# A second staging tile for V, and a new order of work, in a fused attention and gated-unit kernel

## The chip, the cores and the metric

One core of one Trainium2 chip runs the whole program. The metric is the device time of one execution in microseconds (us), median over several runs. The names of the engines in the profile are PE (TensorE, matrix products; PEld is its weight load), DVE (VectorE), ACT (ScalarE), POOL (GpSimd) and SP (SyncE, which here issues the DMA transfers; SPq is its queue). "Clock" is the mean clock that TensorE was granted, as a share of full speed.

## The reference, cut to what matters

Eight batches, eight heads, 576 positions, head size 64; then a gated unit with a causal convolution of five taps over 512 channels.

```python
def _attn_ref(q, k, v, s):                     # (8, 8, 576, 64), s: (8, 8, 576)
    scores = np.matmul(q, k.transpose(0, 1, 3, 2)) / np.sqrt(D)
    cum = np.cumsum(np.maximum(s, 0.0), axis=-1)
    bias = -(cum[:, :, :, None] - cum[:, :, None, :])
    scores = np.where(causal, -1e9, scores + np.minimum(bias, 0.0))
    ...                                        # softmax
    return np.matmul(attn, v)

def _moe_ref(x, w_val, conv_w, w_out):         # x: (8, 576, 512)
    for k in range(5):
        gate_pre += conv_w[k] * xp[:, k:k + S, :]
    gate = 1.0 / (1.0 + np.exp(-gate_pre))
    return gate * (x @ w_val) @ w_out
```

## The kernel before

The kernel is a list of some thousand small tasks. Each names its engine, a planned duration, a key and the tasks it needs. When the kernel is built, a planner runs the list through a simple model of the engines, always taking the ready task with the lowest key; the order that comes out is the order in which the instructions are written. In the traces each engine works off its own list in that order (ScalarE's 204 instructions stand line by line as planned) and waits where an operand is missing. So a planned duration costs no time by itself. It only decides the order.

```python
    def run(self):                             # the planner
        ...
                if e == "SP":
                    idle_at[e] = now + 0.06                    # issuing a transfer is planned as 0.06 us
                    dma_free = max(dma_free, now + 1.2) + us   # one transfer after the other
                    t["done"] = dma_free + 0.8
                else:
                    idle_at[e] = t["done"] = now + us
        ...
    plan = Plan(dict(P=3, gp=2, th=6, ot=3, qkf=3))            # ot: three output tiles
    ...
    vst = one.tile([128, NKB, 8, 65], FP32, name="vst")        # the one staging tile for V
    ...
    def vprime(eng, b, p):                                     # V of two heads, scaled, to bf16
        h = slice(2 * p, 2 * p + 2)
        eng.tensor_tensor(Vps[b % 2][:, :, h], vst[:, :, h], w[...], ALU.mult)

    def load_v_pair(p):                        # first batch: three transfers for two heads
        for h in (2 * p, 2 * p + 1):
            nc.sync.dma_start(out=vst[:, 0:4, h, 0:64], in_=v[0, h, 0:512, :].rearrange("(i p) d -> p i d", i=4))
        nc.sync.dma_start(out=vst[64:128, 4, HP[p], 0:64], in_=v[0, HP[p], 512:576, :].rearrange("h s d -> s h d"))

    def load_v_block(b, i):                    # later batches: five transfers for eight heads
        n = kbs[i]
        nc.sync.dma_start(out=vst[128 - n:128, i, :, 0:64], in_=v[b, :, kbo[i]:kbo[i] + n, :].rearrange("h s d -> s h d"))
    ...
    plan.total = plan.run()
    with tc.manual_schedule():
        for t in plan.order:
            t["emit"]()
```

Positions 512 to 575 of Q and K (the "tail") are loaded apart from the rest, and the second and third block of scores of every pair of heads need them.

## Time and profile before

| | before |
|---|---|
| time, median of 3 runs | 210.72 us (209.64 to 211.25) |
| span of the profiled execution, clock | 209.3 us, 0.965 |
| busy PE / DVE / ACT / POOL | 175.4 / 178.0 / 163.1 / 161.9 us |
| start of the last evacuation of the output (ScalarE) | 203.44 us |

The prediction below shows the busy times, the chain and the three stretches. First, of the page's slices, TensorE's granted clock in forty equal slices (9 is 90% or more of full speed):

```profile
PEclk9999797599999999999999999999999999999995
```

```profile
12.00:18.00 6.00, 5.28 (x70) 3.94 (x67) 3.58 (x5) 5.62 (x9) 3.92 (x6) 1.00 1.09 265
...
33.00:39.00 6.00, 5.07 (x45) 2.99 (x45) 6.00 (x10) 3.55 (x6) 3.54 (x6) 0.60 1.08 260
```

From 40 to 190 us all four engines are 84% to 97% busy (busy time over the length of the stretch) and TensorE has 0.99 and 1.00 of its full clock.

### The profile page before, as it was taken

How to read it: one execution, taken by the hardware profiler on the slowest of the kernel's cores; microseconds unless marked ns; L12 is line 12 of the kernel's file. 1: busy time of each engine (PE TensorE's matmuls, PEld its weight loads, DVE VectorE, ACT ScalarE, POOL GpSimd, SP SyncE). 2: the span in 40 equal slices, each digit the busy share in tenths (PEclk: the TensorE clock that was granted, in tenths of full speed). 3: DMA queues.
4: the chain of work that ended last, by engine and by line, in shares of the span. 5: the costliest groups of instructions: out<-in, count | busy, mean ns of one | idle time of the engine just before them, and what ended most of it. 6: DMA issues, size and time to landing. Idle time of an engine off the chain costs nothing.

```text
span 209.3 us, 6007 instructions
## 1 busy us (share of the span) xinstructions
PE 175.4 (84%) x2392; PEld 119.4 (57%) x2411; DVE 178.0 (85%) x311; ACT 163.1 (78%) x205; POOL 161.9 (77%) x179
## 2 busy tenths in 40 slices
PE   1697885999969998689899799989899999979950
PEld 0455763475736766367665567565576556645620
DVE  3847969999888998669999999999999998999810
ACT  3279497778999899987996998799987998553330
POOL 4276486499959998999589999967975899999300
PEclk9999797599999999999999999999999999999995
DMA  4999999997999699999999821951149220222551
GB/s 147 238 279 288 361 147 216 354 271 207 244 281 323 138 319 221 323 297 226 222 383 307 190 107 25 184 147 49 54 110 219 81 77 1 99 104 75 180 180 61
DMA packets 69230, 40.48 MB, mean 193 GB/s; under 512 B 47109, under 2 KB 63493, under 8 KB 69194
## 3 DMA queue, kind: packets, MB, share of 16 engines
q1 hardware_dynamic: 69194, 40.01, 72.7%
q8 instruction: 21, 0.34, 0.7%
q14 instruction: 15, 0.12, 0.2%
HBM read 30.57 MB, written 9.44 MB: 191 GB/s over the span
## 4 chain that ended last, share of the span: by engine, by line
DVE 27%; ACT 24%; PE 23%; DMA 8%; issue 8%; SPq 7%; ACTq 0%; DVEq 0%
ACT P L592 13%; DVE gp L647 9%; PE banks L660 8%; DMA qkf<-in_moe_w_val_dram 6%; PE banks L672 6%; DVE xn L623 4%; PE banks L613 4%; ACT QKT L561 4%; ACT th L653 4%; DVE glu L666 3%; DVE gp L649 3%; PE banks L566 3%; SPq L515 3%; SPq L534 2%; ACT ot L677 2%
## 5 line engine op out<-in xcount | busy, mean ns | idle before, releaser
L592 ACT ACTIVATE P<-banks 128x1024 bf16<-128x1024 f32 x96 | 94.8, 1039 | 11.8 <-PE banks L566 9.9
L647 DVE SCALAR_TENSOR_TENSOR gp<-banks,ratio,gp 128x574 f32<-128x574 bf16 (+2 forms) x85 | 67.5, 804 | 2.4 <-POOL gp L645 1.7
L598 POOL TENSOR_SCALAR_AFFINE_SELECT P<-P 128x512 bf16<-128x512 bf16 x64 | 39.6, 640 | 11.3 <-ACT P L592 11.1
L566 PE MATMUL banks<-QKT 64*128 64x128 bf16 (+4 forms) x576 | 38.9, 249 | 8.8 <-ACT P L592 5.6
L660 PE MATMUL banks<-xT,wv 128*128 128x288 bf16 x256 | 41.7, 294 | 2.1 <-DVE glu L666 0.9
L672 PE MATMUL banks<-wo,glu 128*128 128x512 bf16 x141 | 38.3, 379 | 2.5 <-ACT QKT L561 0.8
L528 POOL TENSOR_TENSOR Vp<-vst,w 128x650 bf16<-128x650 f32 x29 | 37.6, 1316 | 1.3 <-DMA vst<-in_v_dram 1.3
L613 PE MATMUL banks<-Vp,P 128*128 128x65 bf16 x960 | 37.3, 198 | 1.3 <-ACT P L592 1.2
L613 PEld LDWEIGHTS <-P 128*128 128x128 bf16 x960 | 35.3, 101 | 5.4 <-issue 2.1
L566 PEld LDWEIGHTS <-QKT 64*128 64x128 bf16 x576 | 20.1, 97 | 27.0 <-issue 20.6
L653 ACT ACTIVATE th<-gp,halfw 128x576 f32<-128x576 f32 x32 | 25.2, 793 | 7.1 <-DVE gp L647 3.6
L660 PEld LDWEIGHTS <-wv 128*128 128x128 bf16 x256 | 22.8, 99 | 13.9 <-issue 6.1
L666 DVE SCALAR_TENSOR_TENSOR glu<-th,banks 128x288 bf16<-128x288 f32 x64 | 28.0, 445 | 1.1 <-PE banks L660 1.0
L623 DVE TENSOR_TENSOR xn<-banks,recs 128x640 bf16<-128x640 f32 x32 | 26.2, 818 | 0.3
L561 ACT COPY QKT<-banks 128x1024 bf16<-128x1024 bf16 x25 | 25.3, 1049 | 1.2 <-PE banks L557 1.1
L677 ACT COPY ot<-banks 128x512 f32<-128x512 f32 (+1 forms) x26 | 15.2, 587 | 11.4 <-PE banks L672 6.9
L672 PEld LDWEIGHTS <-glu 128*128 128x128 bf16 x160 | 14.6, 97 | 15.5 <-issue 2.7
L649 DVE SCALAR_TENSOR_TENSOR gp<-xT,ratio,banks 128x576 f32<-128x576 bf16 x25 | 20.1, 809 | 1.6 <-ACT xT L635 0.9
L644 POOL TENSOR_TENSOR tmp<-xT,ratio 128x576 f32<-128x576 bf16 (+3 forms) x18 | 20.6, 1142 | 1.0 <-ACT xT L635 0.5
L645 POOL TENSOR_TENSOR gp<-tmp,gp 128x573 f32<-128x573 f32 (+2 forms) x11 | 15.7, 1428 | 3.1 <-DVE gp L647 2.3
L631 PE MATMUL banks<-ident,xn 128*128 128x128 bf16 x160 | 14.2, 220 | 2.9 <-DVE xn L623 1.2
L518 POOL CAST qb<-qkf 128x2048 bf16<-128x2048 f32 x7 | 13.2, 1890 | 2.2 <-DMA qkf<-in_q_dram 2.2
(63 smaller groups left out, 169.2 us busy)
## 6 DMA issues: line engine op xcount, KB each, us to landing
out_dram<-ot SPq DMA_DIRECT2D x32, 256.0 KB, 2.9
qkf<-in_q_dram SPq DMA_DIRECT2D x7, 1024.0 KB, 8.5
qkf<-in_k_dram SPq DMA_DIRECT2D x7, 1024.0 KB, 9.9
vst<-in_v_dram SPq DMA_DIRECT2D x28, 256.0 KB, 5.4
vst<-in_v_dram SPq DMA_DIRECT2D x15, 128.0 KB, 4.0
first<-in_q_dram SPq DMA_DIRECT2D x4, 256.0 KB, 3.4
first<-in_k_dram SPq DMA_DIRECT2D x4, 256.0 KB, 3.4
tail<-in_q_dram SPq DMA_DIRECT2D x8, 128.0 KB, 8.7
```

Source lines behind the costliest of these rows:

```text
L528: eng.tensor_tensor(Vps[b % 2][:, :, h], vst[:, :, h], w[:, :, b * 8 + 2 * p:b * 8 + 2 * p + 2].unsqueeze(3).to_broadcast([128, NKB, 2, 65 ...
L561: copy[e](QKTs[b % 2][:, :, p, 0:512].rearrange("d w (x j) -> d w x j", j=4), slot["qt", b, p].rearrange("d w (j x) -> d w x j", j=4))
L566: nc.tensor.matmul(ps[:, hh, c0:c0 + nq], QKTs[b % 2][r, 1, p, k0:k0 + 128], QKTs[b % 2][r, 0, p, q0:q0 + nq], **kw)
L592: nc.scalar.activation(out=slot["Pt", n][:, :, step * 512:(step + 1) * 512], in_=slot["s", n, step], func=AF.Exp, scale=0.125)
L598: nc.gpsimd.affine_select(out=d, in_=d, pattern=[[0, 4], [1, 128]], compare_op=ALU.is_ge, fill=0.0, base=0, channel_multiplier=-1)
L613: nc.tensor.matmul(ps[:, hh, qb * 65:qb * 65 + 65], lhsT, Vps[b % 2][:, kb, 2 * p + hh, :], start=(kb == 0), stop=(kb == qb))
L623: nc.vector.tensor_tensor(xns[b % 2][:, :, p * 128:(p + 1) * 128].rearrange("t g (h d) -> t h g d", h=2), pv[:, :, :, 0:64], recs[:, n].un ...
L647: nc.vector.scalar_tensor_tensor(gp[:, o:S], slot["x", n][:, 0:S - o], r, gp[:, o:S], ALU.mult, ALU.add)
L653: nc.scalar.activation(out=th, in_=slot["g", n], func=AF.Tanh, scale=halfw[:, n % 4, :])
L660: nc.tensor.matmul(ps, wv[:, dc, c * 128:(c + 1) * 128], xTs[b % 2][:, dc, 2 + o:290 + o], start=(dc == 0), stop=(dc == 3))
L666: nc.vector.scalar_tensor_tensor(glus[b % 2][:, c, o], slot["t", n][:, o], 1.0, slot["v", n, hf], ALU.add, ALU.mult)
L672: nc.tensor.matmul(ps, glus[b % 2][:, c, WIN[i]:WIN[i] + 128], wo[:, c, :], start=(c == 0), stop=(c == 3))
```

## The change

Its intent: V of one batch can be loaded while that of the batch before is still being scaled, as there are two staging tiles. To make room, the second lies over five of the eight tiles of the first batch's Q and K. V of the second batch comes in pairs of heads, so that its scaling can begin early. The planner's durations for GpSimd come nearer to what the profile shows (that of VectorE for the first batch's V goes away from it, from 0.85 to 1.4 us, where the traces have 0.84), output tiles go from three to five, and all keys and choices of engine are searched anew under the new plan. The diff, cut to its core:

```diff
-DUE = dict(w=-69.33, lwv=-4.26, ...)
+DUE = dict(lv1=-0.54, lv1d=-8.43, vf=-76.23, lt=4.9, w=-131.75, ...)      # every key is new
-CHOICE = dict(vp0="0100", cast="12200210", te="10001100", ...)
+CHOICE = dict(tailc="2", vp0="0000", cast="01211201", te="00000000", ...)  # 0 and 1 choose the engine
...
-                    idle_at[e] = now + 0.06
                     dma_free = max(dma_free, now + 1.2) + us
+                    idle_at[e] = max(now + 0.06, dma_free - BEHIND)
...
-    plan = Plan(dict(P=3, gp=2, th=6, ot=3, qkf=3))
+    plan = Plan(dict(P=3, gp=2, th=6, ot=5, qkf=3))
...
-    vst = one.tile([128, NKB, 8, 65], FP32, name="vst")
+    vraw = [one.tile([128, NKB * 8 * 65], FP32, name=f"vst{j}") for j in range(2)]
+    vsts = [a.rearrange("p (i h d) -> p i h d", i=NKB, h=8) for a in vraw]
...
-                        f = slot["f", 0, wh, p] = one.tile([128, 2, 256], FP32, name=f"first{p}{wh}")
+                        f = slot["f", 0, wh, p] = (one.tile([128, 2, 256], FP32, name=f"first{i}") if i > 4 else
+                                                   vraw[1][:, i * 512:(i + 1) * 512].rearrange("p (h s) -> p h s", h=2))
...
+            if b == 1:
+                t = add("POOL", 0.7, DUE["vf"], lambda: v_frame(1), [T["cast", 0, i % 2, i // 2] for i in range(5)])
+                ts = [[add("SP", 1.45, DUE["lv1"] + DUE["lv1d"] * p, lambda p=p: load_v_pair(1, p), [t])] for p in range(4)]
...
-                T["vp", b, p] = add("POOL", 1.25, ...
+                T["vp", b, p] = add("POOL", 1.33, ...
-                t = add(("DVE", "POOL"), (0.73, 2.25), ... tap ...
+                t = add(("DVE", "POOL"), (0.73, 2.5), ... tap ...
```

## The prediction

> **What bounds the kernel now.** I read the page first, to see whether one engine is full; then the busy time by stretch, to see where the engines are not full; then the waits, for the ones that the change touches; and last the order of time at both ends. The first line below is the page's busy time, the second its chain by engine.
>
> ```profile
> PE 175.4 (84%) x2392; PEld 119.4 (57%) x2411; DVE 178.0 (85%) x311; ACT 163.1 (78%) x205; POOL 161.9 (77%) x179
> ...
> DVE 27%; ACT 24%; PE 23%; DMA 8%; issue 8%; SPq 7%; ACTq 0%; DVEq 0%
> ```
>
> No engine is full and no one engine owns the chain. VectorE (178.0 us of 209.3) and TensorE (175.4) are nearly level, and ScalarE and GpSimd are some 15 us behind. The busy time in three stretches (columns: stretch, length, then PE, PEld, DVE, ACT, POOL busy, clock, DMA share, GB/s) says where the missing 31.3 us of VectorE are:
>
> ```profile
> 0.00:40.00 40.00, 27.42 (x341) 19.59 (x341) 29.13 (x49) 26.29 (x35) 23.87 (x41) 0.89 0.97 249
> 40.00:190.00 150.00, 136.31 (x1989) 93.50 (x2006) 140.33 (x247) 131.14 (x163) 132.62 (x134) 1.00 0.72 186
> 190.00:210.00 20.00, 11.68 (x66) 6.31 (x65) 8.52 (x17) 5.64 (x9) 5.46 (x5) 0.87 0.38 130
> ```
>
> VectorE idles 10.9 us in the first 40, 9.7 in the 150 of the middle (94% busy) and some 11 in the end. So the middle is held by VectorE, with TensorE at 91%; the start by data (DMA share 0.97, and every engine a quarter to two fifths idle); the end by dependences. The waits that the change touches (who waited for what: total us, times, longest):
>
> ```profile
> ACT ot L677 <- DMA out_dram<-ot: 3.0, 2, 1.8
> ...
> DVE Vp L528 <- DMA vst<-in_v_dram: 2.0, 2, 1.3
> ...
> DVE wv L413 <- DMA qkf<-in_moe_w_val_dram: 1.9, 1, 1.9
> ...
> POOL Vp L528 <- DMA vst<-in_v_dram: 1.3, 2, 0.9
> ```
>
> The V staging tile costs its readers 3.3 us, 2.4 of them in the first 20 us. In the DMA queue's own list the single tile shows as well, since each load of V must wait until the batch before has been scaled, and what stands behind it waits too:
>
> ```profile
> SPq L540 <- POOL Vp L528: 6.9, 4, 2.1
> ...
> SPq L523 <- POOL Vp L528: 4.7, 3, 2.9
> ```
>
> In order of time, the fourth pair's Q (L515) is issued only at 11.97 us, because three V transfers stand between one pair's Q and K and the next pair's; and at the end ScalarE's last two evacuations wait for an output tile to be stored, after TensorE has ended at 201.79:
>
> ```profile
> 11.97 0.59 SPq L515 DMA_DIRECT2D first<-in_q_dram  x1
> ...
> 197.31 4.48 PE L672 MATMUL banks<-wo,glu 128*128 128x512 bf16 x19
> ...
> 201.08 0.59 ACT L677 COPY ot<-banks 128x512 f32<-128x512 f32 x1 [1.26 <-DMA out_dram<-ot]
> 203.44 0.59 ACT L677 COPY ot<-banks 128x512 f32<-128x512 f32 x1 [1.77 <-DMA out_dram<-ot]
> ```
>
> [...] a pair of V takes 1.28 us on GpSimd and 0.84 on VectorE, and a tap takes 1.14 + 1.43 = 2.57 us there and 0.80 here, as it is two instructions there. [...] the trace has one scaling of 2.26 us against a median of 1.28, beside the 2.12 us conversion of the weights on VectorE[...]
>
> **The change part by part.** The kernel's arithmetic, bytes and matrix products stay. What changes is which engine does an operation, in which order, and how long a buffer is held. The planner runs when the kernel is built and only fixes the order, so its constants cost no time themselves.
>
> *Engines.* Counted from the strings of choices, times this trace's means. VectorE: one scaling of V more, +0.84; one first conversion less, -0.42; the first tail's conversion, -0.41; three tail evacuations, -1.27; one Q/K evacuation, -1.22; seven x evacuations (26 to 19), -3.16; two output evacuations (14 to 12), -1.37; three taps more, as GpSimd's fall from 18 to 15, +2.41. Sum -4.6: 178.0 becomes 173.4. ScalarE gets the counterparts: two conversions 1.24, three tails 1.78, one Q/K 1.05, seven x 4.65, two outputs 1.17. Sum +9.9: 163.1 becomes 173.0. GpSimd: one V less -1.28, three taps less -7.7, one conversion less -0.61 and the first tail's more +0.61, the memsets of the second V tile +0.7 (0.16 + 0.52 in the start of this trace). Sum -8.3: 161.9 becomes 153.6. TensorE stays at 175.4. So the fullest engine falls from 178.0 to 175.4, and three engines now stand within 2.5 us of each other. In the middle, where VectorE is 94% busy, I take its 4.6 us less at about half, -2.5 us, because TensorE at 91% and ScalarE with 9.9 us more soon bind in its stead.
>
> *The end.* Output tiles go from three to five. With the two waits gone (1.26 + 1.77), the last evacuation can start when TensorE has ended, 201.8 instead of 203.44. That is on the path that ends last: -1.6 us.
>
> *The start.* In the old order twelve V transfers of 0.47 to 0.63 us on the queue stand among the eight of Q and K. The new keys put all Q and K first (-10.8 to -0.2) and V behind (1.8 to 2.9), so eight issues of about 0.5 us bring the fourth pair's K about 6 us earlier than 12.61. ScalarE's exponentials, spread out until about 29 us now, can be packed closer. Against that the tail's two transfers go ahead of the first Q (about 0.6 us later). The second batch's V comes in twelve transfers in place of five, seven more at about 0.55 = 3.9 us of queue time, in a stretch where DMA is full anyway, and it is asked for early: 1.18 MB more ahead of the value weights is 4.7 us at 249 GB/s, and the first gated product needs those weights. Net I take -2.5 of the 10.9 idle us.
>
> *The second V tile in the middle.* It frees loads from the batch before, but the readers wait only 0.9 us there. The 11.6 us of queue waits are prefetch time and mostly hidden. I count nothing beyond the half microsecond in the sum.
>
> *Measured GpSimd times.* The old plan gave 1.25 us for V and 2.25 for a tap where the trace has 1.28 and 2.57; the new one is nearer, so work planned behind GpSimd should be late less often. ScalarE's wait for GpSimd's taps is 3.3 us in all and VectorE's 1.7; part of it is already in the 2.5 of the middle. I add -0.5 for that and the V tile together.
>
> Sum: -2.5 - 1.6 - 2.5 - 0.5 = -7.1 us. The order is new everywhere and in-order engines lose where the plan is off (it still takes 0.905 us for an exponential that lasts 1.04), so I give 1.6 us back for new waits: about -5.5 us, from 210.7 to 205.2.
>
> **The rivals.** (1) ScalarE becomes the bound. It gains 9.9 us of work, and the plan takes its exponentials as 13% too short, 12.9 us over 96 of them. For: it is on the chain for 24% already and 98 to 100% busy in some stretches. Against: it is idle in the last 20 us for 14 and has 18.9 us of slack in the middle. Result 208 to 211. (2) The start stays held by data: the same bytes must arrive for the first gated product, and early V only pushes the weights back. For: DMA share 0.97. Against: the engines idle there also with Q and K still in the queue. Then only the middle and the end pay: 207 to 208. (3) Everything pays in full, as the new plan is truer: start -5, end -1.6, middle -4.6: 199 to 200.
>
> **Range and chances.** The centre is 205.2; rival 2 is the more likely side to miss on, rival 3 the less. The range that should hold it 8 times in 10 is 201.5 to 209.0. The threshold for faster by over 2% is 206.5, 1.3 us above the centre, and the three old runs alone spread over 1.6 us: faster 0.66, within 2% 0.31, slower 0.03.
>
> **What would show it right or wrong.** Right: no wait of an evacuation for a stored output tile at the end; the last Q or K of the first batch issued before 8 us; VectorE near 173 us, ScalarE near 173, GpSimd near 154; VectorE's idle time in the first 40 us down from 10.9 to about 8. Wrong: ScalarE 95% or more busy from 40 to 190 us with VectorE falling below 92% there (rival 1); the conversion of the value weights later than 29.84 us with TensorE waiting for it (rival 2); queue waits for V gone but the same waits under other names; or new waits of TensorE on GpSimd's scaled V because it is now done late.

## More of the kernel before

Third, in order of time, the first exponential of ScalarE (columns: start, duration, engine, line, operation, out<-in, shape, count, and in brackets the idle time just before and what ended it):

```profile
9.08 1.02 ACT L592 ACTIVATE P<-banks 128x1024 bf16<-128x1024 f32 x1 [0.52 <-PE banks L566]
```

Second, the middle cut at 90 us (columns: stretch, length; busy time and count of PE, PEld, DVE, ACT, POOL; clock; DMA share; GB/s), and two short stretches that will matter:

```profile
40.00:90.00 50.00, 44.32 (x662) 30.84 (x668) 43.52 (x73) 47.05 (x58) 45.05 (x46) 0.99 1.04 261
90.00:190.00 100.00, 91.99 (x1329) 62.66 (x1338) 96.81 (x174) 84.09 (x106) 87.56 (x89) 1.00 0.55 149
```

## The result, and the profile after

| | before | after |
|---|---|---|
| time, median (range), 4 runs each | 210.18 us (209.54 to 211.25) | 217.43 us (216.03 to 218.11) |
| ratio of fast runs, 95% interval | | 1.0331 (1.0259 to 1.0403) |
| span of the profiled execution, clock | 209.3 us, 0.965 | 215.9 us, 0.936 |
| busy PE / DVE / ACT / POOL | 175.4 / 178.0 / 163.1 / 161.9 us | 179.1 / 173.3 / 171.1 / 154.1 us |

Here and below a ratio is the mean time of one kernel's fast runs over that of the other's in the same rounds, so it is not quite the ratio of the medians; for the experiments it leaves the profiled execution out. A run is called slow when it is over 1.5% above the fastest of its kernel. The change is slower: 3.31% of 210.2 is 7.0 us. The result is correct.

The page of the kernel after, its busy time and its chain:

```profile
PE 179.1 (83%) x2411; PEld 122.5 (57%) x2411; DVE 173.3 (80%) x300; ACT 171.1 (79%) x220; POOL 154.1 (71%) x174
...
PE 30%; ACT 25%; DVE 22%; DMA 9%; issue 8%; SPq 2%; POOL 1%; ACTq 0%; DVEq 0%; POOLq 0%
```

The work moved between the engines as counted in the prediction (VectorE 173.4, GpSimd 153.6, ScalarE 173.0). VectorE has 4.7 us less to do, and the span is 6.6 us longer, so VectorE stands idle 11.3 us longer. Where, the stretches say (same columns as before):

```profile
0.00:40.00 40.00, 25.99 (x343) 20.15 (x344) 26.09 (x45) 26.80 (x37) 25.19 (x42) 0.87 0.84 217
40.00:90.00 50.00, 42.61 (x547) 28.91 (x545) 36.71 (x61) 38.40 (x49) 39.87 (x41) 0.86 1.06 260
90.00:190.00 100.00, 92.42 (x1390) 62.55 (x1391) 94.21 (x166) 96.42 (x122) 80.48 (x87) 1.00 0.58 157
```

Three of the 11.3 us lie in the first 40 (13.9 idle against 10.9), and 6.8 between 40 and 90 us, where VectorE is busy 36.7 us against 43.5 and ScalarE 38.4 against 47.1. From 90 us on the engines are nearly as full as before: VectorE 94% (97% before), ScalarE now 96% (84%). So the loss is made before 90 us and carried to the end. TensorE's clock shows something as well:

```profile
PEclk9999758967998599999999999999999999999996
```

In the kernel before the low slices end at 42 us, but for the last one. After, they go on to the slice of 70 to 76 us. The mean clock of a run does not sort the runs (the other three after runs had 0.953 to 0.965 and still 214.3 to 216.4 us of span), so the clock can only be a part.

What waits for what (total us, times, longest) in the kernel after. In the kernel before the first of these was 3.3 us, the second 2.2, the third 1.0, and the fourth didn't exist:

```profile
ACT th L666 <- POOL gp L658: 8.6, 5, 3.4
...
POOL qb L530 <- DMA qkf<-in_q_dram: 6.1, 3, 4.6
...
DVE glu L679 <- PE banks L673: 5.3, 5, 1.9
...
DVE wo L419 <- DMA qkf<-in_moe_w_out_dram: 2.7, 1, 2.7
```

And the two ends. First the start: the queue's first issues, then ScalarE's first full exponential.

```profile
0.81 0.77 SPq L535 DMA_DIRECT2D tail<-in_q_dram  x1
1.63 0.61 SPq L535 DMA_DIRECT2D tail<-in_k_dram  x1
2.29 0.57 SPq L506 DMA_DIRECT2D cw<-in_moe_conv_w_dram  x1
2.90 0.41 SPq L527 DMA_DIRECT2D vst<-in_q_dram  x1
...
7.09 0.47 SPq L527 DMA_DIRECT2D first<-in_k_dram  x1
```

```profile
6.75 0.58 ACT L562 COPY QKT<-banks 128x512 bf16<-128x512 bf16 x1 [4.67 <-PE banks L559]
...
11.44 2.84 ACT L605 ACTIVATE P<-banks 128x1024 bf16<-128x1024 f32 x3
```

The last K of the first batch is issued at 7.09 us, 5.5 us earlier than before. But ScalarE, which works its list in order, has the evacuation of the tail first in it and stands 4.67 us for that. Two conversions of K and one more evacuation also stand in front, the second conversion waiting 1.18 us for its K; the first exponential comes at 11.44 instead of 9.08. Then the end:

```profile
208.06 0.59 ACT L690 COPY ot<-banks 128x512 f32<-128x512 f32 x1 [0.33 <-PE banks L685]
208.92 0.58 ACT L690 COPY ot<-banks 128x512 f32<-128x512 f32 x1 [0.28 <-PE banks L685]
209.79 0.59 ACT L690 COPY ot<-banks 128x512 f32<-128x512 f32 x1 [0.28 <-PE banks L685]
```

Each evacuation follows TensorE by 0.3 us. The waits of 1.26 and 1.77 us for a stored tile are gone, as the prediction said.

**The plan against the chip.** As the order is fixed, each task's planned start can be set against its start in the trace. The difference says how far the chip has fallen behind the plan when it comes to that task. For ScalarE's tasks (us; the first column is the plan's own total):

```
plan time      total |   10    20    30    40    50    60    70    80   120   160   200
before        202.23 | -0.0   0.4   1.9   4.0   3.9   3.4   3.1   3.5   2.6   2.4   4.6
after         203.75 |  2.7   2.5   2.6   3.4   6.6   7.4   7.5   9.3   8.5   8.3   9.5
```

Two things follow. Between 80 and 160 us neither kernel loses anything against its plan, and at the end the kernel after loses about 1 us and the kernel before about 2 (its waits for a stored tile). In the kernel after the loss comes in steps: at the very start, between 40 and 50, and between 70 and 80. And the new plan is 1.5 us longer on paper, though it already has the shorter end. With the changed GpSimd times the old order would take some 206 us on paper (205.4 to 206.4, as VectorE's new time for V is left out or taken in), so by the search's own measure the new order was a gain of about 2 us. The chip made a loss of 7 out of it.

### The profile page after: what moved, and what is told of

It reads as the page before. It is cut to its first block, busy times and chain, and to the rows that moved or that the text cites.

```text
span 215.9 us, 6017 instructions
## 1 busy us (share of the span) xinstructions
PE 179.1 (83%) x2411; PEld 122.5 (57%) x2411; DVE 173.3 (80%) x300; ACT 171.1 (79%) x220; POOL 154.1 (71%) x174
## 4 chain that ended last, share of the span: by engine, by line
PE 30%; ACT 25%; DVE 22%; DMA 9%; issue 8%; SPq 2%; POOL 1%; ACTq 0%; DVEq 0%; POOLq 0%
ACT P L605 17%; PE banks L685 9%; PE banks L626 8%; DVE gp L660 7%; PE banks L673 6%; DVE xn L636 4%; PE banks L579 3%; DMA vst<-in_v_dram 3%; ACT QKT L574 3%; DVE gp L662 3%; DMA qkf<-in_moe_w_out_dram 3%; ACT th L666 3%; DMA vst<-in_k_dram 3%; DVE glu L679 2%; PE banks L570 2%
## 5 line engine op out<-in xcount | busy, mean ns | idle before, releaser
L611 POOL TENSOR_SCALAR_AFFINE_SELECT P<-P 128x512 bf16<-128x512 bf16 x64 | 40.9, 661 | 19.6 <-ACT P L605 19.6
L579 PE MATMUL banks<-QKT 64*128 64x128 bf16 (+4 forms) x576 | 39.4, 254 | 13.9 <-ACT P L605 6.4
L626 PEld LDWEIGHTS <-P 128*128 128x128 bf16 x960 | 36.7, 103 | 7.1 <-issue 3.5
L685 PE MATMUL banks<-wo,glu 128*128 128x512 bf16 x160 | 39.2, 379 | 0.6 <-ACT QKT L574 0.2
L540 POOL TENSOR_TENSOR Vp<-vst,w 128x650 bf16<-128x650 f32 x28 | 35.4, 1282 | 1.2 <-DMA vst<-in_v_dram 1.2
L673 PEld LDWEIGHTS <-wv 128*128 128x128 bf16 x256 | 24.2, 101 | 11.9 <-issue 4.3
L574 ACT COPY QKT<-banks 128x1024 bf16<-128x1024 bf16 x26 | 26.2, 1030 | 5.7 <-PE banks L570 5.6
L690 ACT COPY ot<-banks 128x512 f32<-128x512 f32 (+1 forms) x28 | 16.6, 592 | 10.6 <-PE banks L685 6.8
L662 DVE SCALAR_TENSOR_TENSOR gp<-xT,ratio,banks 128x576 f32<-128x576 bf16 x29 | 23.4, 806 | 0.7
L658 POOL TENSOR_TENSOR gp<-tmp,gp 128x572 f32<-128x572 f32 (+2 forms) x12 | 17.0, 1415 | 3.3 <-DVE gp L660 2.5
L657 POOL TENSOR_TENSOR tmp<-xT,ratio 128x572 f32<-128x572 bf16 (+3 forms) x15 | 17.1, 1142 | 2.4 <-DVE xT L648 1.4
```

The lines of the kernel that those rows point to most:

```text
L540: eng.tensor_tensor(Vps[b % 2][:, :, h], vsts[b % 2][:, :, h], w[:, :, b * 8 + 2 * p:b * 8 + 2 * p + 2].unsqueeze(3).to_broadcast([128, NK ...
L574: copy[e](QKTs[b % 2][:, :, p, 0:512].rearrange("d w (x j) -> d w x j", j=4), slot["qt", b, p].rearrange("d w (j x) -> d w x j", j=4))
L579: nc.tensor.matmul(ps[:, hh, c0:c0 + nq], QKTs[b % 2][r, 1, p, k0:k0 + 128], QKTs[b % 2][r, 0, p, q0:q0 + nq], **kw)
L611: nc.gpsimd.affine_select(out=d, in_=d, pattern=[[0, 4], [1, 128]], compare_op=ALU.is_ge, fill=0.0, base=0, channel_multiplier=-1)
L626: nc.tensor.matmul(ps[:, hh, qb * 65:qb * 65 + 65], lhsT, Vps[b % 2][:, kb, 2 * p + hh, :], start=(kb == 0), stop=(kb == qb))
L673: nc.tensor.matmul(ps, wv[:, dc, c * 128:(c + 1) * 128], xTs[b % 2][:, dc, 2 + o:290 + o], start=(dc == 0), stop=(dc == 3))
```

## The experiments

Eighteen runs. The theories, as they stood at first: **the queue** (T1 in the first expectations): V of the second batch in twelve small transfers keeps the queue busy and holds up what is behind it. **The data**: more bytes early, whatever their form. **The order**: the new order leans on times that the planner has wrong, whatever the data do. Later three shares were taken apart: the start, TensorE's clock, the early data.

Two of the kernels turned out to be programs already run.

### How far two runs of the same program differ

The edit of e4_before_ot5 should have given the kernel before five output tiles. It set the wrong key of a dictionary, and three tiles stayed in use. What gave it away was the trace of e10_both_small, which carries the same edit: the wait for a stored tile was still there.

```profile
199.91 0.58 ACT L689 COPY ot<-banks 128x512 f32<-128x512 f32 x1 [1.29 <-DMA out_dram<-ot]
201.85 0.58 ACT L689 COPY ot<-banks 128x512 f32<-128x512 f32 x1 [1.36 <-DMA out_dram<-ot]
```

So e4_before_ot5 is the kernel before, and e10_both_small is e5_before_two_v; in their traces the instructions of VectorE, ScalarE and GpSimd are the same one by one.

```diff
+        slot["ot", b, i] = ots.setdefault("n", 0) % 5      # the key in use is ("ot", (b, i))
         ot = slot["ot", b, i] = work("ot", (b, i), [128, DM], FP32)
```

> The kernel before with five output tiles in place of three, its instruction order kept. The prediction's step for the end: 1.2 to 1.8 us faster, 208.4 to 209.2, the two waits of ScalarE for stored output tiles gone. The rival (the last store's own time sets the end): within 0.5 us.

> The kernel before in its own order, with only the two parts of the change that need no new order: five output tiles and two staging tiles for V. The parts alone gave ratios 0.993 and 0.997. If they are independent (they act at the end and in the middle): 0.990, about 208.7 us against 210.8. If the second V tile's 0.3% was noise: 0.993. If the end gives back what is gained earlier: 0.997.

Measured: e4_before_ot5 209.44 us (209.3 to 215.1, the highest slow) against 210.87, ratio 0.9931 (0.9896 to 0.9967), although it is the same program. e10_both_small 210.51 us (209.88 to 211.46) against 209.92, ratio 1.0065 (1.0019 to 1.0112), and e5_before_two_v, the same program on another chip, 0.9971. So two runs of one program differ by 0.7% and 0.9%, and the printed intervals are too narrow for differences of that size. Below, a step of under 0.7% (1.5 us) is taken as shown only where the trace shows it too or where several runs agree.

### V of the second batch in fewer transfers, or not at all

e1_v1_blocks keeps the order and loads V of the second batch in five block transfers; e2_v01_blocks does so for the first batch too; e6_no_v1 doesn't load it (a wrong result).

```diff
     def load_v_pair(b, p):
         vst = vsts[b % 2]
+        if b == 1:
+            for i in range(NKB if p == 3 else 0):          # e1; in e6: return
+                load_v_block(b, i)
+            return
```

> The changed kernel, its instruction order kept, but the second batch's V comes in five transfers (by blocks of 128 rows) in place of twelve (by pairs of heads). Theory 1 (the SP queue can't issue the small pieces of V fast enough, the DMA engines run short between 33 and 42 us, and all data behind is late): 2 to 3.5 us faster than the changed kernel, 214 to 215.5 us, DMA share of 33 to 39 us back from about 0.65 to about 1. Theory 2 (the loss is in the order in which the compute engines take their work, and data would not help): within 0.7 us of 217. Theory 3 (the 1.18 MB of V that come early push the weights and the next Q and K back, however they are cut): also within 0.7 us.

> As the run before, and the first batch's V in five transfers too. Theory 1: the second short stretch (12 to 18 us) is filled as well, 4 to 6 us faster than the changed kernel, 211 to 213. Theory 2: within 1 us of 217, or slower, since the first pair of V now lands with the last. Theory 3: as theory 2.

> The changed kernel with the second batch's V not loaded at all (wrong result on purpose; the tile keeps what lay in it). It takes away both the issues and the bytes. Theory 1: 3 to 5 us faster than the changed kernel, little more than with five transfers. Theory 3: 4 to 6 us faster where five transfers bring nothing. Theory 2: within 1 us of 217.

| | median (range) | ratio |
|---|---|---|
| e1_v1_blocks | 219.00 us (217.71 to 220.08) | 1.0372 (1.0311 to 1.0433) |
| e2_v01_blocks | 216.97 us (215.96 to 218.88) | 1.0270 (1.0226 to 1.0314) |
| e6_no_v1 | 215.46 us (213.52 to 217.82, the highest slow) | 1.0252 (1.0178 to 1.0326) |

Fewer transfers brought nothing that stands out of the noise (e1 0.4% slower than the change, e2 0.6% faster); e1 fell outside what each of the theories had expected. In e1 the scaling stood for V, as all blocks must be there before the first pair:

```profile
POOL Vp L540 <- DMA vst<-in_v_dram: 2.7, 1, 2.7
```

So e1 takes the issues away and puts a lateness in their place, and can't judge T1 alone. But without any of these issues and 1.18 MB the kernel gains 0.8%, against the 3.3% that are to be explained, so T1 falls as the main cause. (That ratio counts the slow run and leaves the profiled one out; the three fast runs alone are at 1.0187, a gain of 1.4%.)

What V costs the trace shows as a chain. The output weights are issued behind it, at 37.55 us (33.70 before); VectorE stands for them, TensorE then for VectorE, and ScalarE for TensorE, in the kernel after:

```profile
43.71 1.57 DVE L419 TENSOR_SCALAR wo<-qkf 128x2048 bf16<-128x2048 f32 x1 [2.67 <-DMA qkf<-in_moe_w_out_dram]
45.69 1.47 PE L579 MATMUL banks<-QKT 64*128 64x128 bf16 x16 [2.42 <-DVE glu L679]
46.34 1.94 ACT L605 ACTIVATE P<-banks 128x1024 bf16<-128x1024 f32 x2 [1.69 <-PE banks L579]
```

In e6 the output weights are issued at 26.15 us and VectorE doesn't wait for them.

The pieces of V also go with a thinner stream. In the kernel after, the DMA engines are not full in the two stretches in which V is issued by pairs, where they were full before:

```profile
12.00:18.00 6.00, 4.49 (x59) 3.30 (x57) 3.45 (x5) 6.00 (x10) 3.99 (x6) 1.00 0.86 176
...
33.00:39.00 6.00, 4.98 (x62) 3.67 (x60) 5.63 (x10) 4.04 (x6) 4.77 (x5) 0.87 0.65 146
```

176 and 146 GB/s against 265 and 260. From 33 to 39 us e1 brought the share back to 0.93 (208 GB/s), as T1 expected; the time did not follow. From 12 to 18 us the share says little: e9_scores_twice, unchanged there, has 1.00 (197 GB/s).

### No data at all after the first batch

Both kernels, with Q, K, V and tails of later batches not loaded: the engines work on what the first batch left. Their outputs are wrong, which doesn't matter for the times.

```diff
-                    f = slot["f", b, wh] = work("qkf", (b, wh), [128, 8, 256], FP32)
-                    dma_qk(b, wh, slice(0, 8), f)
+                    slot["f", b, wh] = frs[wh]            # the first batch's tile, already there
...
     def load_tail(b):
+        if b:
+            return
```

> The changed kernel, order kept, with no Q, K, V or tail loaded after the first batch (the later batches work on the first one's data: wrong result on purpose; weights and stores stay). What is left of the loss is then the order and the start. If the loss is data that come later than the plan counts on: 205 to 209 us, and 0 to 3 us from the same cut of the kernel before. If the loss is the order in which the compute engines work: still 4 us or more above the same cut of the kernel before.

> The kernel before with the same cut. Data theory: 204 to 208 us (its own data waits after 20 us are only some 3 us), so it gains less from the cut than the changed kernel does (9 or more). Order theory: it gains as much as the changed kernel, 203 or less.

Measured: n_after 214.86 us (214.60 to 216.65), ratio 1.0252 (1.0176 to 1.0328); n_before 208.61 us (208.01 to 210.75), ratio 0.9955 (0.9867 to 1.0042). With weights and stores alone on the way after the first batch the two orders are still 6.3 us apart by the medians. Leaving the data out is worth 0.8% to the new order and 0.45% to the old one, the latter inside the noise; that the old order would gain so little neither theory had expected. So data are a share of the gap and not its cause, and the data fall as the main theory.

### The parts that need no new order

e5_before_two_v gives the kernel before the second V tile, laid over the first Q and K, in its own order. e11_choices keeps the order of the kernel before and changes only which engine does what, to the choices of the change.

```diff
         if pick:
-            emit = partial(emit, eng)
+            emit = partial(emit, alts[int(CHOSEN[pick[0]][pick[1]])][0])    # e11: planned with the old, run with the new
```

> The kernel before with two V tiles, the second laid over the first Q and K as in the change, its order and its transfers kept. The prediction's step (the second tile alone is worth about nothing; the queue's 11.6 us of waits for scaled V are hidden): within 0.7 us of 210.9. Rival (those waits cost): 1.5 us or more faster.

> The kernel before in its own order, with only the engines chosen as in the change (VectorE 178 to about 173 us of work, ScalarE 163 to 173, GpSimd 162 to 153), so the prediction's middle step by itself. If VectorE's work is what the middle costs: 2.5 us faster (208). If the middle is set by the order in which work meets: same or slower by up to 3 us, as the order was searched for the old choices.

Measured: e5_before_two_v 209.65 us (209.23 to 212.48), the highest slow, ratio 0.9971 (0.9898 to 1.0045), so the second tile by itself is worth nothing that can be seen. e11_choices 236.80 us (235.81 to 237.73), ratio 1.1290 (1.1217 to 1.1362). Its stretch from 90 to 190 us:

```profile
90.00:190.00 100.00, 81.69 (x1231) 55.80 (x1230) 80.00 (x138) 85.52 (x108) 68.09 (x73) 1.00 0.53 135
```

VectorE has 4.9 us less to do than in the kernel before and the program takes 27 us more: from 90 to 190 us no engine is fuller than 86%, each waits for another. My rival allowed for 3 us. Here a choice of engines was worth nothing by itself; it belongs to the order for which it was searched.

### The start

e8_start takes the order of the change and puts the Q and K of the first two pairs ahead of the tail and of the convolution weights, with the first exponential ahead of the tail's evacuation and of the second conversion of K. e16_start2 does it with the transfers in the order of the kernel before: first Q and K, s, convolution weights, tail, then the rest.

```diff
     plan.total = plan.run()
+    first = [2, 3, 4, 1, 0, 5, 6, 7, 8, 9, 10, 11, 12, 21, 20, 22, 23, 25, 30, 34, 15, 16, 26, 13, 17, 18]   # e16
+    plan.order = [plan.order[i] for i in first + [i for i in range(len(plan.order)) if i not in first]]
```

> The changed kernel with the first 26 tasks in another order: Q and K of the first two pairs are issued ahead of the tail and of the convolution weights, and the first score, evacuation and exponential stand ahead of the tail's; nothing else moves. If the start (first exponential at 11.4 us where the plan has 8.8, because the queue issues a transfer in 0.5 us and the plan counts 0.06) is carried to the end: first exponential at about 9 us and 1 to 2.4 us faster than the changed kernel, 215 to 216.4. If later waits swallow it: within 0.7 us of 217.4.

> The changed kernel with the start's transfers in the order of the kernel before (first Q and K, then s and the convolution weights, then the tail), and the first exponential ahead of the tail's evacuation. If the late start (first exponential at 11.4 instead of 9.1 us) is a share of its own: first exponential at 8 to 9 us, the first batch 2 us earlier, 1.5 to 2 us off the total, ratio 1.022 to 1.026. If the slack is used up later: ratio 1.030 to 1.034.

Measured: e8_start 216.19 us (216.00 to 216.94), ratio 1.0295 (1.0244 to 1.0347). The first exponential came at 7.57 us, and the gain was lost again at once. I had put the small convolution weights behind the tail, and VectorE, in order, stood for them, until 12.38 us instead of 5.36:

```profile
12.38 0.18 DVE L510 COPY cwT<-banks 128x20 f32<-128x20 f32 x1 [5.07 <-PE banks L504]
```

e16_start2, where that wait is 1.87 us, measured 215.43 us (214.52 to 216.30), ratio 1.0260 (1.0203 to 1.0317), with its first exponential at

```profile
7.58 1.02 ACT L605 ACTIVATE P<-banks 128x1024 bf16<-128x1024 f32 x1 [0.71 <-PE banks L579]
```

It is behind its plan by 0.6 us at 10 us instead of 2.7. By its ratio the start is a share of about 0.7%, 1.5 us; that is no more than the noise, and rests on the trace.

### TensorE's clock

In the kernel after, at 71 us, sixteen products of 128x288 take twice their time, and VectorE, with nothing else in its list, waits for each. In order of time, TensorE and then VectorE:

```profile
66.80 0.40 PE L579 MATMUL banks<-QKT 64*128 64x64 bf16 x4 [0.64 <-ACT P L591]
67.71 0.40 PE L579 MATMUL banks<-QKT 64*128 64x320 bf16 x4 [0.52 <-ACT P L605]
68.62 0.61 PE L579 MATMUL banks<-QKT 64*128 64x128 bf16 x8 [0.52 <-ACT P L605]
...
70.99 4.02 PE L673 MATMUL banks<-xT,wv 128*128 128x288 bf16 x16
```

```profile
72.17 0.45 DVE L679 SCALAR_TENSOR_TENSOR glu<-th,banks 128x288 bf16<-128x288 f32 x1 [1.90 <-PE banks L673]
73.21 0.45 DVE L679 SCALAR_TENSOR_TENSOR glu<-th,banks 128x288 bf16<-128x288 f32 x1 [0.58 <-PE banks L673]
```

What comes before is a stretch in which TensorE gives a small block of scores to ScalarE, waits until ScalarE has done an exponential, and gives the next. From 65.6 to 68.6 us TensorE was busy 1.17 us of 3.00, no gap was above 0.64 us, and the clock was 1.00; from 68.6 to 71 us the clock was 0.51, and from 71 to 75 us, where the sixteen products are, 0.50. In the experiment below they run at a clock of 1.00, and their 4.02 us become 2.13. e9_scores_twice does the score products of the third batch twice, which changes no result and only keeps TensorE busier in this stretch:

```diff
-        for m, (kb, q0, nq, c0) in enumerate(STEPS[step]):
+        for m, (kb, q0, nq, c0) in enumerate(STEPS[step] * (2 if 8 <= n < 12 else 1)):
```

> The changed kernel with each score product of the third batch done twice into the same place (same result), so that TensorE does not idle while ScalarE works through the exponentials at 60 to 72 us. If TensorE's clock, granted at about half there, is part of the loss (16 value products in 4.0 us at 71 us, where 8 take 1.14 us at full clock): clock near 1 there, the block in about 2.2 us, and 1 to 2 us faster. If not: 0 to 1 us slower from the added products.

Measured: 215.31 us (214.09 to 216.11), ratio 1.0257 (1.0189 to 1.0326). The three stretches, first the kernel after, then the experiment (first busy column PE; clock third from the end):

```profile
64.00:68.00 4.00, 2.65 (x35) 1.29 (x34) 3.86 (x7) 3.11 (x5) 3.95 (x5) 1.00 1.05 346
68.00:71.00 3.00, 1.88 (x21) 0.71 (x16) 2.21 (x3) 3.00 (x4) 3.00 (x5) 0.61 1.30 227
71.00:75.00 4.00, 4.00 (x22) 2.59 (x21) 1.36 (x3) 2.80 (x4) 4.00 (x5) 0.50 0.79 145
```

```profile
64.00:68.00 4.00, 3.01 (x57) 1.97 (x55) 3.83 (x6) 4.00 (x6) 4.00 (x5) 1.00 1.13 323
68.00:71.00 3.00, 2.70 (x29) 1.80 (x29) 1.75 (x4) 3.00 (x4) 3.00 (x5) 1.00 1.17 172
71.00:75.00 4.00, 4.00 (x105) 3.67 (x104) 3.30 (x9) 1.26 (x2) 3.92 (x5) 1.00 0.95 260
```

More work for TensorE, and a shorter program: the clock stays at 1.00, VectorE does 3.30 us of work in the last four instead of 1.36, and the block of products reads

```profile
69.45 2.13 PE L673 MATMUL banks<-xT,wv 128*128 128x288 bf16 x16
```

In these runs the busy time of such a stretch alone does not say whether the clock falls after it. From 64 to 68 us TensorE was busy 2.65 us of 4.00 in the kernel after, and the clock of the next 3 us was 0.61; in e17_start2_twice (below) it was busy 2.49 us of 4.00, and the clock of the next 3 us was 1.00. In the kernel before the clock was 1.00 from 58 to 62 us with 2.45 us of 4.00 busy, and 1.00 from 62 to 66 us. What it takes for the clock to fall was not shown.

### Are these shares separate?

First e12_three, all three cures at once (with the faulty start of e8_start), no better than one alone. That looked like one slack seen three times, until the fault of the start was known. Then without the start (e15_no_data_twice), with the mended start and the doubled scores (e17_start2_twice, result correct), and all three (e18_all). e12, e15 and e18 give wrong results. Their edits are those above, put together.

> The changed kernel with three things at once, wrong on purpose: no Q, K, V or tail loads after the first batch, the first tasks reordered so that the first exponential comes early, and the score products of the third batch done twice to keep TensorE's clock. Alone they gave about 1.6, 0.8 and 1.6 us of the 6.9 us gap. If they are separate shares: 3.5 to 4 us off, ratio about 1.013 to 1.017. If they are one and the same slack seen three times: ratio 1.023 to 1.026. If together they open the whole gap: 1.00 to 1.005.

> The changed kernel, no Q, K, V or tail loads after the first batch and the third batch's score products done twice (wrong on purpose). Alone the two gave 214.9 and 215.3 us. If data and TensorE's clock are separate shares: 1.5 to 2 us below either, about 213, ratio 1.015 to 1.018. If they are the same slack: no better than either, 1.024 to 1.026.

> The changed kernel with the mended start and the third batch's scores twice, result correct. If both are separate shares: 1.5 us below the mended start alone, ratio 1.016 to 1.020. If the doubled scores only help where the start was late: 1.024 to 1.028.

> The changed kernel with all three taken away (wrong on purpose): no Q, K, V or tail loads after the first batch, the third batch's scores twice, the mended start. If the start is a third share: 1 to 1.5 us below the 212.4 without it, ratio 1.004 to 1.007, and what remains against the kernel before without data (ratio 0.9955) is the order's own 1.5 to 2 us. If the start's gain is used up by later waits: ratio 1.011 to 1.013.

| edits on the kernel after | median (range) | ratio to before |
|---|---|---|
| none | 217.43 us (216.03 to 218.11) | 1.0331 (1.0259 to 1.0403) |
| mended start (e16) | 215.43 us (214.52 to 216.30) | 1.0260 (1.0203 to 1.0317) |
| mended start, scores twice (e17) | 214.06 us (213.20 to 215.19) | 1.0146 (1.0096 to 1.0196) |
| scores twice, no data (e15) | 212.37 us (211.88 to 213.93) | 1.0119 (1.0061 to 1.0178) |
| mended start, scores twice, no data (e18) | 211.54 us (210.92 to 213.99) | 1.0019 (0.9974 to 1.0063) |
| faulty start, scores twice, no data (e12) | 215.01 us (214.37 to 215.55) | 1.0271 (1.0207 to 1.0334) |

By these times they are separate. e17 takes 1.85% off the change, where start and clock taken alone took 0.71 and 0.74; e15 takes 2.12%, where data and clock alone took 0.79 and 0.74; e18 takes 3.12%, where the three alone took 2.24. Nothing was lost in putting them together, and the surplus is no more than two runs of one program differ by. All three together, 3.12%, are far outside the noise. Down the first, second, third and fifth rows: the start 0.7%, TensorE's clock 1.1%, the data 1.3%, which is 1.5, 2.4 and 2.7 us of the 7.0 when they are taken away in this order. With the noise found above each of them is good to about 1.5 us; taken alone, clock (e9) and data (n_after, and e6 with only V of the second batch left out) came out smaller, at 0.7 to 0.8% each. The faulty start of e12 costs 1.5% against e15. Why the same slip cost nothing net in e8_start is not shown; there it stood against a gain of the start and against waits for data.

The falling behind the plan shows the same thing, for ScalarE's tasks:

```
plan time            |   10    20    30    40    50    60    70    80   120   160   200
after                |  2.7   2.5   2.6   3.4   6.6   7.4   7.5   9.3   8.5   8.3   9.5
mended start (e16)   |  0.6   1.6   1.7   2.4   3.4   5.5   5.5   6.2   5.4   5.2   6.3
and scores twice     |  0.3   1.5   1.6   2.4   3.5   4.9   5.0   4.9   4.1   3.9   5.0
no second V (e6)     |  1.9   2.7   2.0   3.5   3.4   3.2   3.5   4.8   4.1   3.9   5.0
```

The step at 10 us goes with the start. That between 70 and 80 us is 0.7 to 2.1 us, 1.4 in the mean, in all seven traces of the new order without doubled scores (after, e1, e2, e6, e8, e16, n_after), and each of them has a stretch between 64 and 75 us with the clock at 0.50 to 0.61. In the five with doubled scores (e9, e12, e15, e17, e18) it is -0.1 to 0.7 us, 0.1 in the mean, and the clock is 1.00 there. So the traces give TensorE's clock some 1.4 us, less than the 2.4 of the table. The largest step of the kernel after, 3.2 us between 40 and 50, is gone where V of the second batch isn't loaded (e6): it is the chain shown with e6 (the clock between 45 and 50 us is 1.00 in e6 and 0.50 in the kernel after, so a part may be the clock's). One trace is good to no more than 2 us, though: e9, the same instructions up to the plan's 53 us, has 1.5 there, and its VectorE waits 1.1 us for the output weights instead of 2.7.

What is left for the order by itself: e18_all is at 1.0019 where the kernel before without data is at 0.9955, so 0.64% or 1.3 us, near the 1.5 us by which its plan is longer, though no more than the noise. So the 7.0 us are, as an estimate: start 1.5, clock 2.4, data 2.7 less the 0.9 that they cost the old order too, and 1.3 for the order. If the five output tiles, which are in it, give 1.6 us back at the end as in the trace of the next section, the new order proper is some 3 us longer up to there, even undisturbed; no run shows that by itself. Which of its keys does that, no run tells.

### The end, done rightly

e13_ot5 gives the kernel before five output tiles in truth; e14_ot5_two_v adds the second V tile.

```diff
+        ots.append((b, i))
-        ot = slot["ot", b, i] = work("ot", (b, i), [128, DM], FP32)
+        ot = slot["ot", b, i] = one.tile([128, DM], FP32, name=f"ot{len(ots) % 5}")
```

> The kernel before in its own order, output tiles really five. If the prediction's end step is right: ScalarE's last evacuation no longer waits for a stored tile but follows TensorE directly, 1.6 us less in the trace between the last output product and the end, ratio 0.992. Rival: the last store then only queues behind the ones before it, or the end is set elsewhere: ratio 0.998 to 1.002. Two runs of identical programs in this study differed by up to 0.9%, so the verdict is read from the last 10 us of the trace first.

> The kernel before in its own order with five output tiles and two V tiles, the parts of the change that need no new order. If the end step is right and the second V tile is worth nothing: ratio 0.990 to 0.994. If neither is worth anything: 0.998 to 1.004.

Measured: e13_ot5 209.27 us (208.25 to 212.14, the highest slow) against 211.09, ratio 0.9938 (0.9878 to 0.9997); e14_ot5_two_v 209.72 us (207.29 to 211.21, the highest slow), ratio 0.9993 (0.9935 to 1.0052). As times both are within the noise of the same program, and e14 fell where its expectation had "if neither is worth anything". The trace of e13_ot5 is plainer:

```profile
201.52 0.69 DVE L680 COPY ot<-banks 128x512 f32<-128x512 f32 x1 [2.13 <-PE banks L672]
202.38 0.59 ACT L680 COPY ot<-banks 128x512 f32<-128x512 f32 x1 [1.10 <-PE banks L672]
203.24 0.59 ACT L680 COPY ot<-banks 128x512 f32<-128x512 f32 x1 [0.28 <-PE banks L672]
```

From VectorE's last evacuation to ScalarE's last it is 1.72 us here and 3.34 in the kernel before (203.44 - 200.10), 1.62 us less. e13_ot5 is the one version I would keep.

## Why the prediction was wrong

Predicted were 205.2 us and 66% for faster; it came out at 217.4, 8.4 us outside the range.

- **Engine sums: right** to 2 us on ScalarE, 0.5 on GpSimd and 0.1 on VectorE. TensorE was to stay at 175.4 and came to 179.1, with a clock of 0.936; in e15_no_data_twice, at 0.987, it is 175.1 with the added products in it.
- **The end, -1.6: right** in mechanism, and in size by the trace (1.62 us in e13_ot5; the waits are gone in the kernel after). The whole time of e13_ot5 can't tell it from noise.
- **The second V tile, "nothing beyond the half microsecond": right** (e5_before_two_v 0.9971 and 1.0065 for the same program).
- **The start, -2.5: the step that failed first.** Its mechanism was half right: the last K is issued 5.5 us earlier, and the first batch's last normalization does start 2.2 us earlier (30.0 against 32.2 us). But the step "the tail's two transfers go ahead of the first Q (about 0.6 us later)" counted the issue only. In an in-order list the tail's evacuation and two conversions of K stand ahead of the first exponential, which came 2.4 us later. VectorE's idle time in the first 40 us went from 10.9 to 13.9, where I had written "down to about 8". e16_start2 gives the share: about 1.5 us.
- **V of the second batch, "seven more at about 0.55 = 3.9 us of queue time", and "1.18 MB more ahead of the value weights"**: the right suspect, put ahead of the wrong weights, and wrongly netted against the gain. The twelve issues took from 24.17 to 36.11 us, 11.9 us, where the five of before took 6.7. On the queue of the kernel after an issue of the first batch's Q, K and tail took 0.41 to 0.77 us, and two V issues together 1.14 to 2.87 us (7.60 to 36.11 us); the planner had 0.06 us for one. But the value weights were issued before them, at 22.61 us (16.50 in the kernel before). Their conversion began at 31.47 instead of 29.84, half of the sign I had named for rival 2; the other half did not come, as TensorE did not wait for it, and the first gated product began at 33.1 us instead of 36.0. What V pushed back were the output weights, by 3.9 us (37.55 against 33.70), and VectorE waited 2.7 us for them. The share of the data is 0.8 to 1.3%, 1.7 to 2.7 us.
- **The middle, "I take its 4.6 us less at about half, -2.5 us": wrong in kind.** VectorE was not held by its work there but by what it met. Its 4.7 us less work became idle time, as 6.8 us of idle time were added from 40 to 90 us alone. e11_choices shows what such a sum of busy times is worth without its order: 4.9 us less for VectorE and 27 us more for the program.
- **"So I give 1.6 us back for new waits": mis-sized.** I named the cause (in-order engines lose where the plan is off) and put a small number to it. Against the planned total the kernel before loses 4.6 us and the kernel after 9.5.
- **TensorE at half clock was in no step.** The page before showed 0.89 in the first 40 us and I did not ask what a stretch of waiting for exponentials does to the products behind it (4.02 us for the sixteen at a clock of 0.50, 2.13 at 1.00). Its share is 0.7 to 1.1%, 1.6 to 2.4 us by the times, and some 1.4 by the traces. The clock is low between 45 and 50 us too (0.50 in the kernel after); what that costs was not tested.
- **The rivals.** Rival 1 (ScalarE the bound) shows from 90 us on, at 96.4%, but no time is lost there. Rival 2 (start held by data) is a part, by the output weights and not by the first gated product. Rival 3 fell. None of them allowed for a loss of this size: the highest went to 211.

What stays open: how much of each share would be another's if taken away in another order, and which keys make the new order longer on paper. The range of noise doesn't allow either to be settled with whole-program times.

## What to carry to other kernels

In a program of in-order engines a search over a model finds the order that fits the model, and its gain of 2 us on paper is worth no more than the model's worst error: before trusting such a plan, set its start times against a trace and look for the steps. A busy sum moved from one engine to another is no gain unless you can point to the wait that ends earlier. And run the same program twice under two names: here that moved the ratio by 0.7 to 0.9%, more than most of the effects that one would like to read.
